# Weight sums made by accumulating transfers in DRAM, kept first-layer sums, other signs, and a new order of work

## The chip, the cores and the metric

The kernel runs on one core of one Trainium2 chip. A core has TensorE (PE in the profile, with PEld for the loading of its weights), VectorE (DVE), ScalarE (ACT), GpSimd (POOL) and SyncE (SP), which issues most of the transfers; sixteen DMA engines carry them. The metric is the time on the device in microseconds, the median of several runs. Before the change it is 613.53 us (three runs, 613.44 to 614.0).

## The reference

Input x has 2048 rows of 640 numbers in float32. Two branches are computed from it and mixed by a gate for each row:

```
qkv  = x @ wqkv                      # 32 heads of 20
o    = attention over 8 earlier rows at distances 0, 2, .. 14
a    = o @ wo
h    = x @ w1 + b1                   # 640 -> 1728
b    = (h * tanh(softplus(h))) @ w2  # mish, 1728 -> 640
g    = sigmoid((x * gate_w).sum(-1))
out  = g * a + (1 - g) * b
```

## The kernel before

**Arithmetic.** Each float32 operand is split into a high part that TensorE multiplies at full rate and a low part; a product is then three matmuls, high by high, high by low, low by high (`mm3`, lines 534 to 536). The split is one ACT instruction (line 466) and one subtraction on DVE or POOL (line 469). A buffer with the two halves is called a pair.

**Fewer products.** Most products are done in 2 by 2 blocks with seven products in place of eight (the Winograd form of Strassen's scheme). It needs sums and differences of blocks of the left and of the right operand. They are written t1 to t4 for activations and s1 to s4 for weights. Of a weight in blocks 11, 12, 21 and 22 there are four combinations.

- First layer (x times w1): the 2048 rows are worked in two halves, P = 0 and 1, and w1 in six groups q of columns. `pieces` loads the weights of one group and sums them on DVE or POOL (lines 1096 to 1100 and 1125 to 1128, by the helper at line 1044). In the first half the class Quad pairs two blocks of rows of the weight at once, in the second half Single pairs one. `KIND = 'SSSSSS'` makes all six groups Single in the second half. Each has the steps first, second, m1 to m4, l1 and l2, one PSUM bank or more each.
- qkv: eight units u of columns and rows, with eight slots each; unit 2 and 3 together are done by the class Two in the seven-product form (`PAIRS = {2: (0, 1)}`, `load_first` and `load_second`, steps a1 to c3).
- Second layer (mish times w2), `mlp2`: seven products a, b, c, e, g, d, f (`PRODUCTS`), each over seven blocks kc of 128 rows. Its weights are w2's blocks and their sums. `load_step` loads those of a step at least three steps ahead.
- Output product (o times wo), `wo_part`, for both halves with the same seven products and a fifth block of rows ("+" and "-", weights taken positive or negated).

**The weight sums of the last two products.** `sums_of` is called nine times, once for each of seven blocks of w2 and two of wo, where the order of work has the token `sum`. It loads three buffers of weights, makes three sums (lines 1266 and 1279) and a small fourth one on DVE or POOL and a negated part on ACT (line 1285), and stores five pieces to DRAM (`s_d`, `so_d`), from which `load_step` and `load_weights` read them later. The signs of these sums are such that "b" of the output product, the last step of "b" of the second layer and the fifth block of wo also need negated weights (`load_minus`, `load_stack` with minus, `load_minus_two`).

**Accumulating transfers.** A DMA issued on POOL can add to what lies at its target. The kernel before does so for sums of activations: `plus` (line 955) and `adding` (line 1554, in `wo_part`).

**Who sets the order.** The kernel is written as tasks, each for one engine, with what they wait for and which buffers they take. `Plan.run` plays them through with estimated durations and fixes each engine's order; on the chip each engine then goes through its own list in order and waits where something is not there yet. Tasks for "ANY" go to DVE or POOL. Buffers come from rings and are handed out in the order in which the tasks were made. That order is the text ORDER (lines 260 to 274), a list of tokens such as `q.1.0.l2` or `u.4.7`. BANKS (line 259) says which of two rings of PSUM banks a step uses. Attention runs on DVE beside all of this (lines 591, 594, 637, 641) until the middle of the second layer.

Of the kernel before, what the change touches and what calls it, by code (L numbers as in the profile page):

```python
# [259 lines left out]
ORDER = """  # L260
u.0.5 u.0.4 u.0.7 u.0.6 q.0.0.first wq.1 q.0.0.m1 q.0.0.second sum q.0.0.m3 last.0 q.0.0.m4 u.1.0 u.1.2 pieces.0.1 pieces.0.2 q.0.0.l1 q.0.1.first
u.1.1 q.0.1.second q.0.1.m1 sum q.0.0.m2 q.0.0.l2 wa.2 q.0.2.first q.0.1.m4 q.0.1.m3 u.1.3 u.1.7 u.1.5 q.0.1.m2 pieces.0.3 last.1 q.0.1.l1 q.0.1.l2
p.2.0.a1 u.1.6 u.1.4 pieces.0.4 q.0.2.second x.2.4 q.0.2.m1 x.3.1 q.0.2.m3 p.2.3.a1 p.2.0.a2 q.0.2.m2 p.2.1.a1 p.2.0.a3 pieces.0.5 q.0.2.m4 q.0.2.l2
q.0.2.l1 p.2.2.a1 p.2.1.a2 p.2.3.a2 p.2.2.a2 p.2.1.a3 p.2.3.a3 q.0.3.first x.3.4 p.2.0.b2 p.2.1.b2 p.2.1.b1 q.0.3.m1 p.2.2.a3 p.2.3.b2 p.2.0.b1
q.0.3.m4 p.2.3.b1 q.0.3.second p.2.2.b1 q.0.3.m3 q.0.4.first q.0.3.m2 q.0.4.m1 q.0.3.l2 q.0.3.l1 q.0.4.second p.2.0.c0 q.0.4.m2 q.0.4.m3 p.2.2.c0
x.3.2 x.2.0 p.2.2.b2 wc.2 q.0.5.first q.0.4.m4 q.0.4.l2 q.0.5.m1 p.2.1.c0 q.0.4.l1 x.2.1 p.2.0.c1 p.2.2.c1 p.2.3.c0 x.3.0 q.0.5.m2 p.2.2.c3 q.0.5.m4
q.0.5.l2 q.0.5.second p.2.3.c1 p.2.3.c3 p.2.0.c3 x.2.3 x.2.2 p.2.0.c2 p.2.1.c1 p.2.1.c3 q.0.5.m3 third wq.4 x.3.3 p.2.3.c2 q.0.5.l1 p.2.1.c2 p.2.2.c2
u.4.7 u.4.5 u.4.0 pieces.1.0 rest.0 u.4.6 forms.1.0 sum wq.5 u.4.2 sum u.4.3 q.1.0.first q.1.0.second q.1.0.m1 u.4.1 u.4.4 pieces.1.1 q.1.0.m4
q.1.0.m3 q.1.0.l1 u.5.6 u.5.2 u.5.5 u.5.7 u.5.1 q.1.1.first rest.1 u.5.0 sum pieces.1.2 q.1.1.m1 q.1.0.l2 q.1.0.m2 q.1.1.second wq.6 sum wq.7 u.5.4
q.1.1.m4 q.1.1.m3 u.5.3 q.1.2.first q.1.2.m2 u.6.0 pieces.1.3 u.6.2 q.1.1.l1 q.1.2.m1 q.1.2.second u.6.1 q.1.2.m3 u.6.4 q.1.1.l2 q.1.2.m4 u.6.3 u.6.6  # L270
q.1.3.first q.1.1.m2 u.6.7 u.6.5 pieces.1.4 q.1.2.l2 u.7.4 u.7.1 q.1.3.second q.1.4.first q.1.3.m1 q.1.3.m4 u.7.3 u.7.2 q.1.3.m2 sum u.7.5 sum u.7.7
q.1.3.m3 q.1.2.l1 q.1.4.m1 u.7.6 q.1.3.l1 sum q.1.3.l2 q.1.4.second q.1.4.m4 pieces.1.5 q.1.4.m2 lastw.1 u.7.0 q.1.4.m3 q.1.5.first q.1.4.l2 q.1.5.m1
q.1.5.second q.1.4.l1 q.1.5.m4 q.1.5.m3 rest.2 q.1.5.m2 q.1.5.l2 q.1.5.l1 last.2 last.3 rest.3
# [4 lines left out]
def kernel(ctx: ExitStack, tc: tile.TileContext, x, wq, wo, w1, b1, w2, out):  # L278
# [125 lines left out]
    s_d = [dram.tile([128, 1280], F32, name=f"s{kc}") for kc in range(KH)]  # L404
# [726 lines left out]
    def last_pieces(P):  # L1131
# [7 lines left out]
        if P:  # L1139
            W1["second"] = ws  # L1140
# [864 lines left out]
```

## Time and profile before

| | us |
|---|---|
| median of three runs | 613.53 |
| the profiled execution | 614.11 |
| its span, first to last instruction | 612.3 |
| PE busy | 608.3 |
| DVE busy | 578.6 |
| ACT busy | 387.4 |
| POOL busy | 354.9 |

The span is what the trace covers; the execution is 1.8 us longer. Busy times of engines overlap, so they are compared with the span, not added. Two further lines of the page show how the time is spread over the span, each digit the busy tenths of one of forty slices of 15.3 us:

```profile
DVE  8799998999999999999999999999999999989956
POOL 1666799978788915464579566686359864001000
```

POOL is used until the attention on DVE has ended and hardly after that, since the planner gives tasks for "ANY" to DVE from there on. The transfers use the sixteen DMA engines for 0.78 of the span on the mean, at 240 GB/s. In the views of single lines, an entry such as `x8: 779/815/1143` gives the number of instructions and their shortest, median and longest time in ns.

### The profile page before, as it was taken

How to read it: one execution, taken by the hardware profiler on the slowest of the kernel's cores; microseconds unless marked ns; L12 is line 12 of the kernel's file. 1: busy time of each engine (PE TensorE's matmuls, PEld its weight loads, DVE VectorE, ACT ScalarE, POOL GpSimd, SP SyncE). 2: the span in 40 equal slices, each digit the busy share in tenths (PEclk: the TensorE clock that was granted, in tenths of full speed). 3: DMA queues.
4: the chain of work that ended last, by engine and by line, in shares of the span. 5: the costliest groups of instructions: out<-in, count | busy, mean ns of one | idle time of the engine just before them, and what ended most of it. 6: DMA issues, size and time to landing. Idle time of an engine off the chain costs nothing.

```text
span 612.3 us, 9208 instructions
## 1 busy us (share of the span) xinstructions
PE 608.3 (99%) x2710; PEld 505.7 (83%) x2710; DVE 578.6 (94%) x517; ACT 387.4 (63%) x887; POOL 354.9 (58%) x334
## 2 busy tenths in 40 slices
PE   9999999999999999999999999999999999999997
PEld 7888888888888888888888888888888888888886
DVE  8799998999999999999999999999999999989956
ACT  7678567766897575666656775784966653736520
POOL 1666799978788915464579566686359864001000
PEclk9999999999999999999999999999999999999999
DMA  9764796749788688876888799989798874979913
GB/s 323 227 206 139 239 280 194 269 150 313 278 288 262 188 235 221 257 235 185 225 243 277 226 318 284 346 236 267 232 329 239 231 226 140 279 251 303 279 65 120
DMA packets 101346, 147.01 MB, mean 240 GB/s; under 512 B 11616, under 2 KB 54624, under 8 KB 101072
## 3 DMA queue, kind: packets, MB, share of 16 engines
q1 hardware_dynamic: 97936, 140.66, 71.1%
q0 software_dynamic: 3072, 5.51, 6.4%
q8 instruction: 21, 0.34, 0.3%
q14 instruction: 29, 0.24, 0.1%
q10 hardware_dynamic: 288, 0.26, 0.1%
HBM read 92.38 MB, written 53.03 MB: 237 GB/s over the span
## 4 chain that ended last, share of the span: by engine, by line
PE 97%; ACT 1%; DVE 1%; issue 0%; POOL 0%
PE qb L534 16%; PE qb L535 16%; PE qb L536 16%; PE sb L535 16%; PE sb L536 16%; PE sb L534 16%; PE qb L698 1%; DVE raw L1044 1%; ACT pair L466 1%; PE sb L442 1%; PE sb L540 0%; PE qb L541 0%; PE sb L541 0%; PE qb L540 0%; POOL raw L1044 0%
## 5 line engine op out<-in xcount | busy, mean ns | idle before, releaser
L469 POOL TENSOR_TENSOR pair<-raw,pair 128x512 fp32r<-128x512 f32 (+3 forms) x136 | 169.5, 1269 | 69.0 <-ACT pair L466 46.9
L466 ACT ACTIVATE pair<-raw 128x512 fp32r<-128x512 f32 (+3 forms) x235 | 137.1, 611 | 53.9 <-DMA raw<-actt 12.6
L536 PE MATMUL sb<-pair,pair 128*128 128x512 f32 (+1 forms) x396 | 153.0, 386 | 0.0
L534 PE MATMUL sb<-pair,pair 128*128 128x512 f32 (+1 forms) x396 | 153.0, 386 | 0.0
L535 PE MATMUL sb<-pair,pair 128*128 128x512 f32 (+1 forms) x396 | 153.0, 386 | 0.0
L534 PE MATMUL qb<-pair,pair 128*128 128x512 f32 (+1 forms) x377 | 145.6, 386 | 0.0
L535 PE MATMUL qb<-pair,pair 128*128 128x512 f32 (+1 forms) x377 | 145.5, 386 | 0.0
L536 PE MATMUL qb<-pair,pair 128*128 128x512 f32 (+1 forms) x377 | 145.4, 386 | 0.0
L591 DVE TENSOR_TENSOR pr<-kvq,qg 128x2560 f32<-128x2560 f32 x32 | 89.8, 2807 | 3.3 <-ACT qg L597 2.3
L637 DVE TENSOR_TENSOR pr<-kvq,pg 128x2560 f32<-128x2560 f32 x32 | 90.2, 2820 | 1.0
L594 DVE TENSOR_REDUCE lg<-pr 128x128 f32<-128x2560 f32 x32 | 90.2, 2818 | 0.7
L641 DVE TENSOR_REDUCE kvq<-pr 128x320 f32<-128x2560 f32 x32 | 90.0, 2814 | 0.4
L534 PEld LDWEIGHTS sb<-pair,pair 128*128 128x128 f32 x396 | 74.3, 188 | 14.9
L535 PEld LDWEIGHTS sb<-pair,pair 128*128 128x128 f32 x396 | 74.3, 188 | 14.8
L536 PEld LDWEIGHTS sb<-pair,pair 128*128 128x128 f32 x396 | 74.3, 188 | 14.7
L534 PEld LDWEIGHTS qb<-pair,pair 128*128 128x128 f32 x377 | 70.8, 188 | 14.4 <-ACT qb L1171 0.5
L536 PEld LDWEIGHTS qb<-pair,pair 128*128 128x128 f32 x377 | 70.8, 188 | 13.8
L535 PEld LDWEIGHTS qb<-pair,pair 128*128 128x128 f32 x377 | 70.8, 188 | 13.7
L469 DVE TENSOR_TENSOR pair<-raw,pair 128x512 fp32r<-128x512 f32 (+3 forms) x99 | 68.6, 714 | 3.7 <-ACT pair L466 3.5
L1044 POOL TENSOR_TENSOR hb<-hb,hb 128x512 f32<-128x512 f32 x42 | 55.0, 1327 | 11.7 <-ACT hb L1177 4.8
L1044 POOL TENSOR_TENSOR raw<-raw,raw 128x128 f32<-128x128 f32 (+3 forms) x49 | 40.5, 840 | 12.9 <-DMA raw<-in_wq 2.9
L469 POOL TENSOR_TENSOR pair<-hb,pair 128x512 fp32r<-128x512 f32 (+2 forms) x29 | 34.9, 1210 | 15.7 <-DMA act<-hb 5.8
(173 smaller groups left out, 755.1 us busy)
## 6 DMA issues: line engine op xcount, KB each, us to landing
actt<-hb SPq DMA_DIRECT2D x52, 256.0 KB, 4.0
raw<-in_w SPq DMA_DIRECT2D x40, 256.0 KB, 4.0
act<-hb SPq DMA_DIRECT2D x38, 256.0 KB, 4.2
raw<-actt SPq DMA_DIRECT2D x37, 256.0 KB, 2.6
raw<-in_wq SPq DMA_DIRECT2D x36, 248.0 KB, 4.0
raw<-act SPq DMA_DIRECT2D x29, 256.0 KB, 4.4
raw<-in_x SPq DMA_DIRECT2D x27, 256.0 KB, 4.0
o<-ot SPq DMA_DIRECT2D x64, 80.0 KB, 3.2
```

The source lines that it names most:

```text
L442: nc.tensor.matmul(warm_banks[i % 3].t[:, :n], ones[:, :128], ones[:, :n], start=i < WARM, stop=True, skip_group_check=True)
L466: a = add("ACT", act_ns(n), lambda: A.activation(hi(), raw(), AF.Copy), after, rank=rank, take=take, hold=hold)
L469: return (V if e == "DVE" else G).tensor_tensor(lo(), raw(), hi().bitcast(F32), op=OP.subtract)
L534: nc.tensor.matmul(ps, ah, bh, start=first, stop=False, skip_group_check=more)
L535: nc.tensor.matmul(ps, ah, bl, start=False, stop=False, skip_group_check=more)
L536: nc.tensor.matmul(ps, al, bh, start=False, stop=last, skip_group_check=more)
L591: return V.tensor_tensor(pr, window(kv, s0, 0), qg[:, :, None, :].to_broadcast([128, 2, W, QF]), op=OP.mult)
L594: V.tensor_reduce(lg_w[:, s0:s0 + 2], pr.rearrange("p s w (h d) -> p s w h d", d=DH), op=OP.add, axis=AX.X)
L637: V.tensor_tensor(pairs.rearrange("p s k i (h d) -> p s k i h d", d=DH), vw, pg[:, s0:s0 + 2].rearrange("p s (k i) h -> p s k i h", i=2)[: ...
L641: V.tensor_reduce(q[:, s0:s0 + 2], pairs.rearrange("p s k i f -> p s f k i"), op=OP.add, axis=AX.XY)
L698: nc.tensor.matmul(ps.t[:, :n], X[0, kc].t[:, a, i * 128:(i + 1) * 128], WQ[0, kc].t[:, b, :n], start=a == b and kc == 0, stop=False)
L1044: return (V if e == "DVE" else G).tensor_tensor(t.t[:, i:i + n], a.t[:, j:j + n], b.t[:, k:k + n], op=op)
```

## The change

1. `sums_of` is a new function. For each of w2 and wo it makes four tensors that cover all blocks at once, each with one copy from DRAM to DRAM on SP's queue and one accumulating DMA on POOL's queue. The nth is started when a PE task has ended: for w2 the step l2 of the second half's group n - 1, for wo the nth product of the second layer. The tokens `sum` that are left in ORDER do nothing.
2. w2 and wo are laid out anew by the host (two halves; 256 columns of all blocks, then 128, then 256), wo's fifth block is an input of its own, wo4. A weight block of 384 columns is then two DMAs of 256 and 128 columns (`load_parts`, `block`).
3. The signs of the sums are others. t3 and t4 of the second layer's activations are turned round, several additions of the second layer and of `wo_part` become subtractions and the reverse, and the negated fifth block of wo is dropped; "d" and "f" of the output product and one step of "d" and "f" of the second layer take negated weights in its place. After the second layer's "d", DVE reads the PSUM bank itself, where ACT copied it to a buffer before.
4. The first half's `pieces` stores its sums to DRAM, and the second half's loads them in place of making them (four sums of 128 columns for each group). The same is written for the class Two (`keep`, `kept_raw`), for a unit 6 in PAIRS, which PAIRS does not have.
5. ORDER and BANKS are new.

```diff
 ORDER = """
-u.0.5 u.0.4 u.0.7 u.0.6 q.0.0.first wq.1 q.0.0.m1 q.0.0.second sum q.0.0.m3 last.0 q.0.0.m4 u.1.0 u.1.2 pieces.0.1 pieces.0.2 q.0.0.l1 q.0.1.first
+u.0.5 pieces.0.1 u.0.7 q.0.0.first u.0.6 u.0.4 wq.1 q.0.0.second q.0.1.first last.0 u.1.1 q.0.1.m1 pieces.0.2 wa.2 q.0.0.m1 pieces.0.3 q.0.0.m2
...
-    s_d = [dram.tile([128, 1280], F32, name=f"s{kc}") for kc in range(KH)]
+    s_d = {n: dram.tile([128, KH * (256 if n == 1 else 384)], F32, name=f"s{n}") for n in (1, 2, 3, 4)}
...
-        if P:
+        if P and KIND[q] == "S":
             ra, rb, rc = [raw_buf() for _ in range(3)]
...
-            dc = dma(lambda: rc.t[:, 256:384], lambda: w1[b][:, 0], take=[rc], size=65536)
-            s1 = combined(128, (rc, 384), (rc, 256), (rb, 128), OP.add, [db, dc], rank=SOON)
-            s3 = combined(128, (rc, 256), (ra, 0), (rc, 256), OP.subtract, [da, s1], rank=SOON)
-            s2 = combined(128, (rc, 0), (rc, 384), (ra, 0), OP.subtract, [da, s1], rank=SOON)
-            s4 = combined(128, (rc, 128), (ra, 256), (rc, 0), OP.subtract, [s2], rank=SOON)
-            PIECES[P, q] = [split_pair(ra, 512, [da]), split_pair(rb, 512, [db]), split_pair(rc, 512, [s4, s3])]
+            dc = dma(lambda: rc.t, lambda: w1s_d[q, 0], kept_sums[q], take=[rc])
+            PIECES[P, q] = [split_pair(ra, 512, [da]), split_pair(rb, 512, [db]), split_pair(rc, 512, [dc])]
...
+                kept_sums[q] = [dma(lambda i=i: w1s_d[q, 0][:, i * 256:(i + 1) * 256].rearrange("p (k f) -> p k f", f=128),
+                                    lambda r=r: r.t.rearrange("p (k f) -> p k f", f=256)[:, :, :128], w, rank=1.0, hold=[r], size=131072)
+                                for i, r, w in ((0, o1, [s4]), (1, rb, [s3]))]
...
+    def let_go(P, q, t):
+        if P and q < 4:
+            sums_of(w2, KH, s_d, "s", 1 + q, t)
...
+    def sums_of(w, k, to, key, n, at):
+
+        a1, a1r, a2 = k * 256, k * 384, k * 640
+        first = {1: lambda: w[0][:, a1r:a2], 2: lambda: w[0][:, :a1r], 3: lambda: w[0][:, :a1r], 4: lambda: w[1][:, :a1r]}[n]
+        more, wide = {1: (lambda: w[1][:, a1r:a2], a1), 2: (lambda: to[1], a1), 3: (lambda: w[0][:, a1r:a2], a1), 4: (lambda: to[2], a1r)}[n]
+        c = dma(lambda: to[n], first, [at], rank=0.5, size=512 * (a1 if n == 1 else a1r))
+        before = done[key, n // 2] if n % 2 == 0 else []
+        done[key, n] = [add("POOL", 900, lambda: G.dma_start(out=to[n][:, :wide], in_=more(), accum_op=OP.add, max_dma_last_dim=2048), [c] + before,
+                            rank=-0.5, size=1024 * wide, late=1500)]
+
+    def load_parts(srcs, after=(), minus=False, wide=True):
...
+    def block(of, k, i):
+
+        return [(256, lambda: of()[:, i * 256:(i + 1) * 256]), (128, lambda: of()[:, k * 256 + i * 128:k * 256 + (i + 1) * 128])]
...
                     elif name == "d":
-                        z = stage(True)
-                        read["v", P, j] = c = copy(z, bank["v", P, j], [ends["d", "v", P, j]], [z])
                         b = zw[key]
-                        v = two("ANY", b, b, z, OP.add, [c, b.done])
-                        y[key].used = v = two("ANY", b, y[key], b, OP.subtract, [v, y[key].done])
+                        read["v", P, j] = v = two("DVE", b, bank["v", P, j], b, OP.subtract, [ends["d", "v", P, j], b.done])
+                        y[key].used = v = two("ANY", b, y[key], b, OP.add, [v, y[key].done])
                         result(b, 2 * P + 1, 2 + j, [v])
...
+                if k < 4:
+                    sums_of(wo, 2, so_d, "so", 1 + k, last)
...
     def load_last_weights():
-        weights["-"] = load_minus_two([lambda: wo[4][:, :256], lambda: wo[4][:, 384:]])
-        weights["+"] = load_two([lambda: wo[4][:, :256], lambda: wo[4][:, 384:]], [])
-        weights["4"] = load_pair(lambda: wo[4][:, 256:384], "ANY", n=128, wide=True)
+        weights["+"] = load_parts([(256, lambda: wo4[:, :256]), (256, lambda: wo4[:, 384:])])
+        weights["4"] = load_pair(lambda: wo4[:, 256:384], "ANY", n=128, wide=True)
...
         def l2(self):
             t = self.mms(self.de, self.one(1, 1, self.form("t4")) + self.plain(1, 0), [self.sd])
+            let_go(self.P, self.q, t)
             self.acted(1, 0, self.de, [t])
...
-        elif kind == "sum":
-            sums_of(*sums_left.pop(0))
```

More of the change, by code (lines that the diff above doesn't have):

```diff
@@ L265 @@
[L265 to L268, printed above, removed]
@@ L274, with kernel @@
+q.1.4.m1 q.1.3.l1 q.1.4.m4 q.1.4.m3 q.1.3.l2 sum q.1.4.l2 q.1.5.first q.1.5.second sum wq.7 q.1.5.m2 u.7.2 q.1.5.m1 u.7.7 u.7.3 q.1.4.l1 q.1.4.m2 sum
+q.1.5.m4 q.1.5.l2 lastw.1 last.2 q.1.5.m3 q.1.5.l1 u.7.5 u.7.1 last.3 rest.1 u.7.6 u.7.4 u.7.0 rest.2 rest.3
 """
 @with_exitstack
-def kernel(ctx: ExitStack, tc: tile.TileContext, x, wq, wo, w1, b1, w2, out):
+def kernel(ctx: ExitStack, tc: tile.TileContext, x, wq, wo, wo4, w1, b1, w2, out):
     nc = tc.nc
@@ L803, in plain_weights, with keep, kept_raw @@
                 self.w["r", half, kc] = split_pair(r, n, [d])
+        def keep(self, name, i, r, after):
+            if self.P or i not in PAIRS.get(6, ()):
+                return []
+            kept_sums[name, i] = [dma(lambda: wqs_d[name, i][:, :NCOL], lambda: r.t[:, :NCOL], after, rank=1.0, hold=[r], size=NCOL * 512)]
+            return kept_sums[name, i]
+        def kept_raw(self, name, i):
+            r = raw_buf()
+            self.w[name, i] = split_pair(r, self.n, [dma(lambda: r.t[:, :NCOL], lambda: wqs_d[name, i][:, :NCOL], kept_sums[name, i], take=[r], size=NCOL * 512)])
         def load_first(self):
@@ new lines, in load_parts, with parts @@
+    def load_parts(srcs, after=(), minus=False, wide=True):
+        raw, p, n = stage(wide), pair_buf(), sum(m for m, _ in srcs)
+        def parts():
+            at = 0
+            for m, src in srcs:
+                nc.sync.dma_start(raw.t[:, at:at + m], src())
+                at += m
+        d = add("SP", 450 * len(srcs), parts, after, take=[raw], size=n * 512)
+        if minus:
+            a = add("ACT", act_ns(n), lambda: A.activation(p.t[:, 0, :n], raw.t[:, :n], AF.Copy, scale=-1.0), [d], rank=SOON, take=[p], hold=[raw])
+            b = add("DVE", dve_ns(n), lambda: V.scalar_tensor_tensor(p.t[:, 1, :n], raw.t[:, :n], -1.0, p.t[:, 0, :n].bitcast(F32),
+                    op0=OP.mult, op1=OP.subtract), [a], rank=SOON, hold=[raw, p])
+            p.ready = [a, b]
+        else:
+            p.ready = split(lambda: raw.t[:, :n], lambda: p.t[:, 0, :n], lambda: p.t[:, 1, :n], n, [d], "ANY", [raw], [p], SOON)
+        return p
@@ L1459, in after_product @@
                         z = y[key] = zp[key]
-                        z.done = two("DVE", z, z, bank["u", P, j], OP.add, [ends["c", "u", P, j], z.done])
+                        z.done = two("DVE", z, bank["u", P, j], z, OP.subtract, [ends["c", "u", P, j], z.done])
                     elif name == "e":
@@ L1475, in after_product @@
                         b = y[key]
-                        result(b, 2 * P, 2 + j, [two("DVE", b, b, bank["v", P, j], OP.subtract, [ends["f", "v", P, j], b.used])])
+                        result(b, 2 * P, 2 + j, [two("DVE", b, b, bank["v", P, j], OP.add, [ends["f", "v", P, j], b.used])])
                 if name in "bd":
@@ L1732, in wo_part @@
         for j in range(2):
-            y[j].done = two("DVE", y[j], y[j], bank[f"u{j}"], OP.add, [ends[f"u{j}"], y[j].done])
+            y[j].done = two("DVE", y[j], bank[f"u{j}"], y[j], OP.subtract, [ends[f"u{j}"], y[j].done])
         for j in range(2):
```

206 lines of the change are left out of this document (87 added, 119 removed).

## The prediction

> **What bounds the kernel now.** The page comes first, its head and its first part (busy time, share of the span, number of instructions). Then the busy time of each engine by stage: a row has the stretch, its length, then busy us and number of instructions of PE, PEld, DVE, ACT and POOL, the granted clock, the share of the DMA engines and GB/s.
>
> ```profile
> span 612.3 us, 9208 instructions
> PE 608.3 (99%) x2710; PEld 505.7 (83%) x2710; DVE 578.6 (94%) x517; ACT 387.4 (63%) x887; POOL 354.9 (58%) x334
> ```
>
> ```profile
> 60.00:220.00 160.00, 160.00 (x714) 133.44 (x713) 153.73 (x106) 111.89 (x283) 129.13 (x114) 1.00 0.77 245
> 220.00:378.00 158.00, 158.00 (x709) 132.86 (x708) 154.57 (x112) 102.54 (x244) 97.45 (x101) 1.00 0.83 245
> 378.00:434.00 56.00, 56.00 (x249) 46.37 (x248) 54.85 (x40) 38.44 (x79) 35.96 (x32) 1.00 0.90 275
> 434.00:546.00 112.00, 112.00 (x495) 92.74 (x495) 108.96 (x121) 65.56 (x134) 57.67 (x50) 1.00 0.79 239
> 546.00:580.00 34.00, 34.00 (x151) 28.15 (x150) 33.39 (x57) 19.59 (x35) 2.49 (x3) 1.00 0.96 289
> ```
>
> TensorE is busy for the whole of every stage at a granted clock of 1.00. DVE stands close behind, but it is not what ends last. A busy PE need not be a PE at its pace, so the next view is PE's timeline (start, length, line, tiles, shape) at the only places where two matmuls start more than 0.26 us apart once the start-up is over.
>
> ```profile
> 35.11 0.39 PE L536 MATMUL sb<-pair,pair 128*128 128x512 f32 x1
> 35.55 0.50 PE L534 MATMUL qb<-pair,pair 128*128 128x512 f32 x1
> 35.89 0.40 PE L535 MATMUL qb<-pair,pair 128*128 128x512 f32 x1
> 36.12 0.39 PE L536 MATMUL qb<-pair,pair 128*128 128x512 f32 x1
> ```
>
> ```profile
> 75.66 0.38 PE L535 MATMUL qb<-pair,pair 128*128 128x496 f32 x1
> 75.88 0.38 PE L536 MATMUL qb<-pair,pair 128*128 128x496 f32 x1
> 76.24 0.50 PE L534 MATMUL qb<-kvq,pair 128*128 128x512 f32 x1
> 76.58 0.39 PE L535 MATMUL qb<-kvq,pair 128*128 128x512 f32 x1
> ```
>
> ```profile
> 146.97 0.39 PE L536 MATMUL qb<-pair,pair 128*128 128x512 f32 x1
> 147.33 0.50 PE L534 MATMUL qb<-kvq,pair 128*128 128x512 f32 x1
> 147.67 0.40 PE L535 MATMUL qb<-kvq,pair 128*128 128x512 f32 x1
> ```
>
> The pace is the distance of two starts: 36.12 - 35.89 = 0.23 us for 512 columns, 75.88 - 75.66 = 0.22 us for 496. From 35.11 to 35.89 two steps took 0.78 us instead of 0.45, so 0.33 us were lost. From 75.88 to 76.58 it was 0.70 instead of 0.45, and from 146.97 to 147.67 the same: 0.25 us each. **All the waiting of PE after its start is 0.33 + 0.25 + 0.25 = 0.83 us.** The view of waits names what ended the three:
>
> ```profile
> PEld qb L534 <- ACT qb L1171: 0.5, 1, 0.5
> PEld qb L534 <- ACT hb L1177: 0.4, 1, 0.4
> PEld qb L534 <- ACT hx L708: 0.4, 1, 0.4
> ```
>
> Each time a weight load waited for an ACT instruction that had to read a PSUM bank first. No wait for a DMA, for POOL or for DVE reaches PE. What is left of the span lies behind the last matmul:
>
> ```profile
> 608.91 0.28 PE L536 MATMUL qb<-pair,pair 128*128 128x256 f32 x1
> 609.23 0.42 DVE L1707 TENSOR_TENSOR kvq<-kvq,qb 128x256 f32<-128x256 f32 x1 [0.54 <-PE qb L536]
> ```
>
> From 609.2 to 612.3 the last half block is added and sent: 3.1 us, in the order that the change also has.
>
> So the time is PE's stream plus its ends. The profiled execution took 614.11 us, 1.8 more than its span; the median of the three runs is 613.53, that is 0.58 below the profiled one. I take the same 0.58 off any sum.
>
> **The change, part by part.**
>
> *PE.* The edits touch neither mm3 (lines 534 to 536) nor mm2 (540, 541), nor PRODUCTS, KIND and PAIRS, which set how many products there are. A ("-", ...) becomes ("+", ...) with the same matmul. 2710 matmuls remain, of the same widths: 0 us. A gain can only come out of the 0.83 us, so the best case is 613.53 - 0.83 = 612.7 us. That is 0.14% and less than the 0.2% (1.23 us) which a measurement of this kernel can tell from no change.
>
> *Weight sums off POOL.* These are two answers of the busy time over the whole span for single lines: 1266, then 1279, the sums of w2 and wo. Behind them stand the 128x128 sums of the second half's pieces (from the groups: number, busy us, mean ns, idle time before them).
>
> ```profile
> 0.00:613.00 613.00, 18.00 (x27) 1.00 0.78 240
> 0.00:613.00 613.00, 11.97 (x9) 1.00 0.78 240
> ```
>
> ```profile
> L1044 POOL TENSOR_TENSOR raw<-raw,raw 128x128 f32<-128x128 f32 x19 | 8.8, 476 | 6.3 <-DMA actt<-hb 2.3 <-DVE hb L1044 1.6 <-DVE ot L547 1.3
> L1044 DVE TENSOR_TENSOR raw<-raw,raw 128x128 f32<-128x128 f32 x5 | 2.0, 406 | 0.0
> ```
>
> POOL loses 18.0 + 12.0 + 8.8 = 38.8 us of its 354.9, DVE 2.0 us, and ACT nine small negations. POOL is 58% busy and releases no matmul late, so this is worth 0 on the path: the 99% of PE hides it. Were PE not there, DVE with 94% would be next, and it loses only the 2.0 us.
>
> *Accumulating transfers.* In their place come four copies on SP's queue and four accumulating DMAs on POOL's for w2, and as many small ones for wo. The issue of such a DMA on POOL, and its time from issue to landing:
>
> ```profile
> L1554 POOL DMA_DIRECT2D ot<-ot x8: 779/815/1143, 239.3 to 571.4; - x8
> DMA to landing us min/median/max: 4.0/5.7/7.7
> ```
>
> These move 128x512 (0.262 MB). The new ones move 1792, 1792, 1792 and 2688 columns for w2 (4.13 MB) and 512, 512, 512 and 768 for wo (1.18 MB). No row shows an issue of that size. Low end: a fixed 0.81 us each, 6.5 us for eight. High end: in step with the bytes, 5.31 / 0.262 x 0.81 = 16.4 us. Nothing excludes either; I take 8 us, near the row, as the rows differ in partitions but not in time. POOL still ends with 22 to 32 us less work.
>
> *DMA engines.* The queues' rows give prices:
>
> ```profile
> q1 hardware_dynamic: 97936, 140.66, 71.1%
> q0 software_dynamic: 3072, 5.51, 6.4%
> ```
>
> Two rows of the sums' tensor, their stores and the first loads of a sum (number, ns min/median/max, first and last start in us), place them in time:
>
> ```profile
> L499 SPq DMA_DIRECT2D s<-raw x35: 319/382/1905, 42.7 to 319.1; - x35
> L1320 SPq DMA_DIRECT2D hb<-s x5: 377/430/1179, 408.0 to 447.8; - x5
> ```
>
> On q1 1 MB costs 0.711 x 612.3 / 140.66 = 3.1 us of all sixteen engines, on q0, which only accumulates, 0.064 x 612.3 / 5.51 = 7.1 us. Removed: nine times 0.655 MB in and out, 11.8 MB, 36.5 us. Added: accumulates 5.31 MB x 7.1 = 37.7 us; copies 6.49 MB x 3.1 = 20.1 us; twelve stores of 0.131 MB for the kept pieces and six loads longer by 0.197 MB, 2.75 MB, 8.5 us. Net +30 us in 612, so the mean share goes from 0.78 to about 0.83. The sums of w2 now all fall into the second half of the first layer (row 220:378, share 0.83) instead of being spread from 42.7 us on. The largest accumulate is 1.38 MB, 9.8 us of all engines. A load of SP's queue that shares them for all of that time can land up to 10 us late.
>
> What hides this: in the second layer loads run three steps ahead, and a step is 18 matmuls of 0.227 us, 4.1 us, so 12 us. The sums themselves are not urgent: they start when a PE task of the second half ends, and the first load of one was issued at 408.0 us.
>
> The Trainium skill says on this point, in "DMA: Bandwidth & Descriptors", section "Issuing engines are not separate DMA queues", that DMAs of all issuing engines end on the same 16 engines and interleave. By that rule the accumulates take turns with the loads, which is the contention above; no row of this trace isolates it.
>
> *SP's queue.* 72 issues go (nine sums with three loads and five stores). 8 copies, 12 stores and 24 further issues for weights that are now read in two blocks come. 28 fewer, so the queue gains slack: 0.
>
> *Signs.* The second layer's "d" loses four ACT copies to DVE reading the bank itself; wo loses one negated weight. This follows the product's end and no matmul waits for it in the trace: 0. The bank is read by DVE instead of ACT, and DVE is fuller. The end of this is that a bank could come free late, by one DVE instruction of 2.8 us at most (attention's), but attention is over by then:
>
> ```profile
> 511.93 2.82 DVE L641 TENSOR_REDUCE kvq<-pr 128x320 f32<-128x2560 f32 x1
> ```
>
> *keep and kept_raw* act only if PAIRS has a unit 6. It has not: 0.
>
> *The new list* sets another order of all PE work in the first layer and other PSUM rings. Its cost is the waits at its own hand-overs. The low end is none (-0.83 us). The high end is what several waits of the seen size or one long one make: ten of 0.3 us are +3 us. The nearest rows are the three waits, so I take about as many, 0.7 us.
>
> **Sum:** 613.53 - 0.83 + 0.7 = 613.4 us.
>
> **The rivals.**
>
> 1. *POOL stands still for a copy (slower).* The accumulate sits in POOL's queue and waits there for its copy, and everything behind it on POOL, above all the low halves of line 469 that PE multiplies by, waits too. The trace has such waits:
>
> ```profile
> POOL o L1554 <- DMA o<-ot: 45.3, 1, 45.3
> POOL actt L955 <- DMA act<-hb: 6.3, 1, 6.3
> ```
>
> The long one falls after 512 us, when nothing else was put on POOL, so it cost nothing. A copy of 1.38 MB takes 4.3 us alone and 8 to 9 beside equal traffic. This decides once the wait is longer than the lead of the low halves queued behind it, some 4 us for one step. Then three copies of this size with 1 us too much each give +3 us, 616.4. Against it: POOL has 42% idle, and the mean of its work per us falls. Chance 0.14.
>
> There is a rule that would make this worse: the Trainium skill, "SBUF — State Buffer", section "SBUF: two separate sides", says that while DVE runs an instruction which takes the port shared with GpSimd, GpSimd can't write descriptors. By it each of eight issues would wait for one DVE instruction of 2.82 us, 22 us of POOL. The trace does not agree: issues took 0.779 to 1.143 us beside a DVE that is 94% busy. So it does not raise the chance.
>
> 2. *The list waits at other places (slower).* ACT releases PE at all three waits; in another order a bank is read late more often. It decides from five further waits of 0.25 us (1.25 us). Six to eight give 615. Against it: three in 2710 matmuls is what the order before shows. Chance 0.11.
>
> 3. *Faster by over 0.2%.* It would need 1.23 us, where 0.83 are to be had. Only a shorter tail or start could add to it, and neither is edited. Chance 0.03, about 612.2.
>
> 4. *The change does not do what it says* (the sums land as before in effect, only elsewhere): then nothing moves on PE, 613.5. It falls together with the forecast.
>
> **How the numbers follow.** The forecast, PE's stream unchanged and waits under 2 us in all, has 0.72: 613.4 us, by itself 612.7 to 614.7. Slower is 0.14 + 0.11 = 0.25, faster 0.03. The range goes from the floor, 612.7, up to 616.0, which takes in the list's rival and the nearer half of POOL's; outside stay some 0.03 below and 0.12 above.
>
> **What would show it.** Right: PE still has 2710 matmuls and about 608 us busy; no gaps of over 0.26 us beyond a handful; POOL falls to about 325 us; q0 grows to about 10.8 MB and 12 to 13% of the engines. Wrong: waits of PE for POOL's low halves (line 469) right behind an accumulate; or waits for DMA between 220 and 378 us. The forecast would be wrong at its root if the span fell below 611.5 us, as PE's stream itself would then have become shorter.

## The result, and the profile after

| | before | after |
|---|---|---|
| median, us | 613.76 (613.44 to 614.3, 4 runs) | 618.15 (617.88 to 618.51, 4 runs) |
| ratio | | 1.0071, 95% interval 1.0054 to 1.0088 |
| profiled execution, us | 614.11, span 612.3 | 618.51, span 616.7 |

The changed kernel is 4.4 us slower. That is outside the predicted range (612.7 to 616.0) and on the other side of its 613.4. The page of the changed kernel, its head and its two queues:

```profile
span 616.7 us, 9053 instructions
...
PE 609.4 (99%) x2710; PEld 504.7 (82%) x2710; DVE 579.1 (94%) x516; ACT 392.3 (64%) x879; POOL 322.9 (52%) x282
...
q1 hardware_dynamic: 91728, 137.84, 68.1%
q0 software_dynamic: 5984, 10.82, 11.4%
```

PE has the same 2710 matmuls and is busy for about as long, and POOL lost 32 us: the work is what was foreseen. The busy time by stage (start and end, length, busy us of PE, PEld, DVE, ACT, POOL, granted clock, DMA share, GB/s) shows where PE is not filled any more:

```profile
20.00:60.00 40.00, 38.62 (x169) 31.09 (x168) 32.05 (x30) 25.75 (x60) 24.00 (x21) 1.00 0.65 198
60.00:220.00 160.00, 158.26 (x701) 130.91 (x700) 157.50 (x110) 116.00 (x281) 109.95 (x92) 1.00 0.74 232
220.00:378.00 158.00, 158.00 (x708) 132.72 (x708) 154.33 (x106) 104.27 (x243) 81.14 (x69) 1.00 0.88 249
434.00:546.00 112.00, 112.00 (x496) 92.78 (x495) 110.90 (x127) 69.09 (x139) 54.64 (x49) 1.00 0.92 284
```

The stages in which the accumulating transfers run, from 220 us on, are full, although their DMA share rose (0.83 to 0.88, and 0.79 to 0.92 in the last row). The two stages ahead of them are not. The view of waits of PE's weight loads names who released it (us in total, times, longest); the start-up and two rows of 0.2 us are left out:

```profile
PEld sb L537 <- ACT sb L936: 1.5, 2, 1.1
PEld sb L539 <- DVE pair L472: 1.2, 1, 1.2
PEld qb L537 <- DVE hb L1234: 0.9, 1, 0.9
PEld sb L537 <- DVE sb L883: 0.9, 1, 0.9
PEld sb L537 <- ACT hb L997: 0.7, 1, 0.7
PEld qb L537 <- ACT qb L1216: 0.7, 1, 0.7
PEld sb L538 <- POOL pair L472: 0.4, 1, 0.4
```

Before there were three such rows, of 0.4 and 0.5 us, all for ACT. (Lines 534 to 536 are now 537 to 539, low half 469 is 472, high half 466 is 469, sum 1044 is 1074.)

To add them up I counted, in PE's timeline from 6 us on, each place where two matmuls start more than 0.26 us apart, as the distance less a pace of 0.225 us. This table holds that count, in us, for every trace that is spoken of below (in brackets the number of the experiment):

| kernel | 6 to 60 us | 60 to 90 | 90 to 160 | 160 to 200 | from 200 | all |
|---|---|---|---|---|---|---|
| before | 0.32 | 0.25 | 0.24 | 0 | 0 | 0.8 |
| after | 2.21 | 0.80 | 0.11 | 2.22 | 0 | 5.3 |
| after, no stores (1) | 1.69 | 0.80 | 0.10 | 2.21 | 0 | 4.8 |
| after, no accumulating sums (2) | 2.44 | 0 | 0.08 | 2.21 | 0 | 4.7 |
| after with the old list (3) | 0 | 0 | 3.05 | 5.95 | 29.20 | 38.2 |
| before with the new list (4) | 1.12 | 0.75 | 0.77 | 17.53 | 16.48 | 36.7 |
| after, early sums on DVE (5) | 0.18 | 0.98 | 0.10 | 2.22 | 0 | 3.5 |
| before, a multiplication twice (6) | 4.85 | 0 | 0.25 | 0 | 0 | 5.1 |
| after, a multiplication twice (7) | 4.92 | 0.81 | 0.10 | 2.22 | 1.24 | 9.3 |
| after, no stores, early sums on DVE (8) | 0.16 | 0.83 | 0.10 | 2.21 | 0.52 | 3.8 |
| after, no multiplication at 163 us (9) | 3.81 | 0 | 0 | 1.48 | 0 | 5.3 |
| after, no stores (10) | 1.80 | 0 | 0.10 | 2.21 | 1.06 | 5.2 |
| after, as 5 and 9, copy of line 936 on DVE (11) | 0.45 | 0.72 | 0.10 | 2.71 | 0 | 4.0 |

From before to after 4.5 us came up, against 4.4 us between the two profiled executions. The match is closer than the count deserves: the first 6 us lie outside it, and the start differs from trace to trace. The 85th matmul starts at 20.61 us before and at 19.93 us after, and among the variants of the changed kernel between 19.85 and 20.98 us. **There are two places: up to 90 us, +2.4 us, and 167 to 185 us, +2.2 us.** Behind 185 us the changed kernel's PE never waits. The second place came out at 2.21 or 2.22 us in all seven traces that leave list, code and work there as they are (after, 1, 2, 5, 7, 8 and 10). The first is not as steady: experiments 2 and 9 issue the same instructions as the changed kernel up to 160 us, and lost 2.4 and 3.8 us up to 90 us where it lost 3.0.

**The first place.** PE's timeline (start, length, line, tiles, shape, in brackets the idle time before it and who ended it):

```profile
38.08 0.50 PE L539 MATMUL sb<-kvq,pair 128*128 128x512 f32 x1 [0.76 <-DVE pair L472]
...
43.01 0.50 PE L537 MATMUL qb<-pair,pair 128*128 128x512 f32 x1 [0.31 <-ACT qb L1216]
...
48.38 0.50 PE L537 MATMUL sb<-pair,pair 128*128 128x512 f32 x1 [0.31 <-ACT hb L997]
```

DVE's timeline at that place, then POOL's and ACT's:

```profile
34.44 4.73 DVE L472 TENSOR_TENSOR pair<-raw,pair 128x512 fp32r<-128x512 f32 x5
41.04 1.31 DVE L472 TENSOR_TENSOR pair<-raw,pair 128x512 fp32r<-128x512 f32 x1 [1.87 <-issue]
42.27 2.81 DVE L594 TENSOR_TENSOR pr<-kvq,qg 128x2560 f32<-128x2560 f32 x1
```

```profile
36.41 3.35 POOL L1074 TENSOR_TENSOR raw<-raw,raw 128x256 f32<-128x256 f32 x3
...
47.36 0.74 POOL L1074 TENSOR_TENSOR raw<-raw,raw 128x256 f32<-128x256 f32 x1
```

```profile
39.80 1.15 ACT L469 ACTIVATE pair<-raw 128x512 fp32r<-128x512 f32 x2 [2.66 <-POOL raw L1074]
...
41.36 0.44 ACT L600 ACTIVATE qg<-kvq 128x320 f32<-128x320 f32 x1
...
42.34 0.61 ACT L1216 ACTIVATE qb<-sb 128x512 f32<-128x512 f32 x1
```

Five low halves take DVE 0.95 us each, and three sums take POOL 1.12 us each, while both run; another such sum took POOL 0.74 us. PE, at 37 us, waits for one of the five. ACT stands for 2.66 us until POOL's sums are done, then the copy of line 600 and the seed of line 1216 (the copy into the PSUM bank from which PE goes on) come behind, and PE waits for that seed at 43 us. The third wait, at 48 us, is for ACT's instruction of line 997. A fourth, at 79 us (0.69 us, the row of line 1234), is for a sum of DVE; it is missing in experiments 2, 9 and 10. The first multiplication of attention starts at 42.27 us. Before it was here:

```profile
35.13 2.81 DVE L591 TENSOR_TENSOR pr<-kvq,qg 128x2560 f32<-128x2560 f32 x1
```

**The second place**, ACT's timeline and the matmul that waited:

```profile
165.59 0.68 ACT L1222 ACTIVATE hb<-sb,bias 128x512 f32<-128x512 f32 x1
166.16 1.63 ACT L469 ACTIVATE pair<-raw 128x496 fp32r<-128x496 f32 x3
167.68 0.58 ACT L936 ACTIVATE sb<-pair 128x496 f32<-128x496 f32 x1
```

```profile
168.32 0.49 PE L537 MATMUL sb<-pair,pair 128*128 128x496 f32 x1 [0.64 <-ACT sb L936]
...
172.01 0.49 PE L537 MATMUL sb<-pair,pair 128*128 128x496 f32 x1 [0.53 <-DVE sb L883]
```

The copy that seeds PE's bank (line 936) has no idle time of ACT ahead of it: three high halves stand in the queue before it. 3.7 us later PE waits again, for a subtraction of DVE, and at 185 us for 0.20 us, again for a copy of line 936.

### The profile page after: what moved, and what is told of

Read it like the earlier page. It is cut to its first block, busy times and chain, and to the rows that moved or that the text cites. A ratio compares the mean times of both kernels' runs of the same rounds, so it can differ in the third digit from the quotient of the medians.

```text
span 616.7 us, 9053 instructions
## 1 busy us (share of the span) xinstructions
PE 609.4 (99%) x2710; PEld 504.7 (82%) x2710; DVE 579.1 (94%) x516; ACT 392.3 (64%) x879; POOL 322.9 (52%) x282
## 4 chain that ended last, share of the span: by engine, by line
PE 88%; DVE 6%; DMA 2%; ACT 1%; issue 1%; POOL 1%; SPq 0%; POOLq 0%; DVEq 0%
PE sb L537 15%; PE sb L538 15%; PE sb L539 15%; PE qb L537 13%; PE qb L538 13%; PE qb L539 13%; DVE lg L597 2%; DVE pr L594 2%; DVE pair L472 1%; DMA raw<-in_wq 1%; DMA raw<-in_w 1%; POOL raw L1074 1%; PE qb L701 1%; DVE pr L640 0%; DVE hb L1234 0%
## 5 line engine op out<-in xcount | busy, mean ns | idle before, releaser
L472 POOL TENSOR_TENSOR pair<-raw,pair 128x512 fp32r<-128x512 f32 (+3 forms) x133 | 167.8, 1287 | 101.7 <-ACT pair L469 59.8
L469 ACT ACTIVATE pair<-raw 128x512 fp32r<-128x512 f32 (+3 forms) x230 | 135.5, 613 | 71.4 <-DMA raw<-actt 11.9
L537 PE MATMUL sb<-pair,pair 128*128 128x512 f32 (+1 forms) x406 | 157.3, 387 | 1.5 <-ACT sb L936 0.6
L538 PE MATMUL sb<-pair,pair 128*128 128x512 f32 (+1 forms) x406 | 156.9, 386 | 0.0
L539 PE MATMUL sb<-pair,pair 128*128 128x512 f32 (+1 forms) x406 | 156.8, 386 | 0.0
L537 PE MATMUL qb<-pair,pair 128*128 128x512 f32 (+2 forms) x367 | 141.9, 387 | 0.3 <-ACT qb L1216 0.3
L538 PE MATMUL qb<-pair,pair 128*128 128x512 f32 (+2 forms) x367 | 141.7, 386 | 0.0
L539 PE MATMUL qb<-pair,pair 128*128 128x512 f32 (+2 forms) x367 | 141.7, 386 | 0.0
L537 PEld LDWEIGHTS sb<-pair,pair 128*128 128x128 f32 x406 | 76.2, 188 | 18.2 <-ACT sb L936 1.5
L538 PEld LDWEIGHTS sb<-pair,pair 128*128 128x128 f32 x406 | 76.2, 188 | 15.2 <-POOL pair L472 0.4
L539 PEld LDWEIGHTS sb<-pair,pair 128*128 128x128 f32 x406 | 76.2, 188 | 15.0
L537 PEld LDWEIGHTS qb<-pair,pair 128*128 128x128 f32 x367 | 68.9, 188 | 14.5 <-ACT qb L1216 0.7
L539 PEld LDWEIGHTS qb<-pair,pair 128*128 128x128 f32 x367 | 68.9, 188 | 13.5
L538 PEld LDWEIGHTS qb<-pair,pair 128*128 128x128 f32 x367 | 68.9, 188 | 13.4
L472 DVE TENSOR_TENSOR pair<-raw,pair 128x512 fp32r<-128x512 f32 (+2 forms) x97 | 70.5, 755 | 6.2 <-ACT pair L469 4.1
L1074 POOL TENSOR_TENSOR hb<-hb,hb 128x512 f32<-128x512 f32 x44 | 57.1, 1314 | 27.9 <-DVE pg L630 8.9
L469 ACT ACTIVATE pair<-hb 128x512 fp32r<-128x512 f32 (+3 forms) x63 | 37.6, 598 | 12.0 <-DMA hb<-in_w 4.8
```

The lines of the kernel that those rows point to most:

```text
L469: a = add("ACT", act_ns(n), lambda: A.activation(hi(), raw(), AF.Copy), after, rank=rank, take=take, hold=hold)
L472: return (V if e == "DVE" else G).tensor_tensor(lo(), raw(), hi().bitcast(F32), op=OP.subtract)
L537: nc.tensor.matmul(ps, ah, bh, start=first, stop=False, skip_group_check=more)
L538: nc.tensor.matmul(ps, ah, bl, start=False, stop=False, skip_group_check=more)
L539: nc.tensor.matmul(ps, al, bh, start=False, stop=last, skip_group_check=more)
L1074: return (V if e == "DVE" else G).tensor_tensor(t.t[:, i:i + n], a.t[:, j:j + n], b.t[:, k:k + n], op=op)
```

## The experiments

Theories: **the list** (A), the new order of PE's work makes hand-overs that DVE and ACT serve too late; **the transfers** (B), the new stores or accumulates hold back a load, POOL or SP; and within A, **lateness** (A1: DVE is behind, and PE pays for it) against **the hand-over itself** (A2: it is too tight whether DVE is behind or not).

**1. Without the stores of the first-layer sums.**

```diff
-            dc = dma(lambda: rc.t, lambda: w1s_d[q, 0], kept_sums[q], take=[rc])
+            dc = dma(lambda: many(rc), lambda: w1[b][:, :4], kept_sums[q], take=[rc])
...
+                kept_sums[q] = [add("SP", 450, lambda: None, w, rank=1.0, hold=[r], size=131072) for r, w in ((o1, [s4]), (rb, [s3]))]
```

> The changed kernel, with every engine's order of work as it is, but the twelve stores of kept first-layer sums are planned and not issued; the second half's loads read w1 itself in their place (so its first layer is computed from other weights). After the change PE loses about 2.2 us between 36.9 and 48.4 us, right behind the first two stores. If those stores cause it, by holding raw buffers which the loads of x for the forms need next, these gaps shrink to under 0.7 us and the time is about 616.3 us. If the list causes it, the gaps stay and the time is 618.1 us, as after the change. The waits around 167 to 172 us stay by both theories.

617.27 us (616.95 to 618.29), ratio 1.0051 [1.0034, 1.0068]. It lies between, and its interval overlaps that of the change. In its trace two of the three waits up to 60 us are gone, and the first, for the low half, grew from 0.93 to 1.39 us.

**2. Without the accumulating sums.**

```diff
-        c = dma(lambda: to[n], first, [at], rank=0.5, size=512 * (a1 if n == 1 else a1r))
+        c = add("SP", 450, lambda: None, [at], rank=0.5, size=512 * (a1 if n == 1 else a1r))
...
-        done[key, n] = [add("POOL", 900, lambda: G.dma_start(out=to[n][:, :wide], in_=more(), accum_op=OP.add, max_dma_last_dim=2048), [c] + before,
+        done[key, n] = [add("POOL", 900, lambda: None, [c] + before,
```

> The changed kernel with every engine's order as it is, but the eight copies and eight accumulating transfers of the weight sums are planned and not issued; the second layer and the output product read plain blocks of w2 and wo in the place of the sums. If the accumulating transfers cost time (POOL standing still behind a copy, or loads sharing the DMA engines), the time falls towards 614 to 616 us and waits of PE after 185 us go away. If the list costs it, 618.1 us as after the change, since all of PE's waits lie before 185 us and the first transfer of the sums starts later.

618.38 us (617.62 to 618.86), ratio 1.007 [1.0055, 1.0085]: as with them. **5.3 MB of accumulates and their copies cost nothing that these runs can tell**, and in the changed kernel PE has no wait behind 185 us that they could have caused; the first copy is issued at 228 us.

**3 and 4. Each list with the other code.** The edit exchanges ORDER and BANKS.

> The changed kernel with ORDER and BANKS of before. If the code is free and the new list alone costs the 4.4 us, this gives 613 to 614 us. If the code costs them, 618 us. If a list fits only the code that it was made for, both theories on single parts fail and it is far above 618 us, 625 us or more, with waits of PE all over the first layer.

> The kernel before with ORDER and BANKS of the change. If the new list alone costs the 4.4 us, this gives about 618 us. If the code does, 613.5 us. If a list fits only the code that it was made for, it is far above 618 us, 625 us or more.

652.11 us and 650.3 us, one run each. The first is 34 us over the changed kernel, the second 36.5 us over the one before, so the totals don't divide the 4.4 us between code and list. They show that a list fits the code that it was made for.

Up to 90 us the traces do divide it. With the old list PE loses 0.57 us there under the old code and nothing under the new one; with the new list it loses 1.87 us under the old code and 3.01 us under the new one. Attention begins on DVE at 35.13 and 33.68 us with the old list, at 40.76 and 42.27 us with the new one. These are its first multiplications in experiment 3, then in 4:

```profile
33.68 2.81 DVE L594 TENSOR_TENSOR pr<-kvq,qg 128x2560 f32<-128x2560 f32 x1
```

```profile
40.76 2.82 DVE L591 TENSOR_TENSOR pr<-kvq,qg 128x2560 f32<-128x2560 f32 x1 [0.35 <-ACT qg L597]
```

**So the first place comes with the new list, whichever code runs under it** (one trace each). Six of the twelve stores of first-layer sums are issued before 60 us under the old list too, and PE waits for nothing. Behind 90 us the two runs wait at places of their own, so whether list or code makes the second place stays open.

**5. The early combinations on DVE alone.**

```diff
-                    ins = t.fn(e) if t.both else t.fn()
+                    ins = t.fn("DVE" if e == "POOL" and now < 41000 else e) if t.both else t.fn()
```

> The changed kernel with the same order of work, but what POOL does of additions and low halves before about 41 us is issued on DVE at the same place of the order. After the change DVE instructions with two operands take 1.2 to 1.8 us where a POOL instruction runs beside them and 0.69 alone, and the attention on DVE begins at 42.3 us, 35.1 before. Theory A: this mutual hold-up in the first 42 us sets how late DVE is from then on, and PE's waits up to 185 us follow from it. Then DVE's early instructions fall to 0.69 us, the attention begins 2 to 3 us earlier, PE's waits shrink by 1 to 2 us and the time is 616 to 617 us. Theory B: the list's waits have nothing to do with DVE being late: 618.1 us. Theory C: DVE, with more to do, becomes later still: over 619 us.

616.95 us (616.64 to 618.46), ratio 1.0055 [1.004, 1.007]. The groups of 8 to 42 us by form (number, busy us, mean ns, idle time before), first in the changed kernel, then here:

```profile
L472 DVE TENSOR_TENSOR pair<-raw,pair 128x512 fp32r<-128x512 f32 x19 | 17.4, 956 | 5.6 <-ACT pair L469 3.7 <-issue 1.9
```

```profile
L472 DVE TENSOR_TENSOR pair<-raw,pair 128x512 fp32r<-128x512 f32 x22 | 14.5, 688 | 5.4 <-ACT pair L469 5.4
L1074 DVE TENSOR_TENSOR raw<-raw,raw 128x512 f32<-128x512 f32 x8 | 5.5, 688 | 0.2
```

With POOL out of the way a low half takes 688 ns instead of 956, and DVE does more of them in less time. Attention begins earlier, and PE's waits up to 60 us fall from 2.21 to 0.18 us:

```profile
38.85 2.82 DVE L594 TENSOR_TENSOR pr<-kvq,qg 128x2560 f32<-128x2560 f32 x1
```

So lateness is what PE pays for up to 60 us; 0.18, 0.16 and 0.45 us in the three traces with this edit (5, 8 and 11) stand against 1.69 to 3.81 us in the five without it (after, 1, 2, 9 and 10). The edit takes away two latenesses at once, DVE's slow low halves and POOL's sums that ACT stood still for, and does not divide them. The Trainium skill, "SBUF — State Buffer", section "SBUF: two separate sides", says that a DVE instruction with two SBUF inputs and a GpSimd instruction that reads SBUF exclude each other. The 688 and 956 ns agree that they hold each other up, not that they exclude each other wholly: in the 2.76 us from 36.41 to 39.17 us, when both ran, about 2.9 low halves and 2.5 sums were done, 3.8 us of work by 0.688 and 0.74 us each (my estimate from the rows above), and there the measurement decides. But the hold-up isn't what the change added. Before had the same hold-up, in the same view of 8 to 42 us:

```profile
L469 DVE TENSOR_TENSOR pair<-raw,pair 128x512 fp32r<-128x512 f32 x15 | 12.9, 869 | 1.9 <-ACT pair L466 1.6
L1044 DVE TENSOR_TENSOR raw<-raw,raw 128x512 f32<-128x512 f32 x5 | 6.7, 1348 | 0.0
```

That is 15 x 0.18 + 5 x 0.66 = 6.0 us of DVE lost, against 19 x 0.27 = 5.1 us after. The old list had the room for it. Of the 7.14 us by which attention begins later (42.27 against 35.13), 3.42 went with POOL's work; 3.72 us stay, and experiments 3 and 4 give them to the new order.

**6 and 7. A multiplication of attention twice**, the first one, in the kernel before and in the changed one.

```diff
-                return V.tensor_tensor(pr, window(kv, s0, 0), qg[:, :, None, :].to_broadcast([128, 2, W, QF]), op=OP.mult)
+                for _ in range(2 if (u, s0) == (0, 6) else 1):
+                    ins = V.tensor_tensor(pr, window(kv, s0, 0), qg[:, :, None, :].to_broadcast([128, 2, W, QF]), op=OP.mult)
+                return ins
```

> The kernel before with the first attention multiplication on DVE issued twice, 2.82 us more on DVE at 35 us and nothing else. Theory A: the order of before has less room than that, PE then waits as after the change, mostly between 70 and 190 us: 615.5 to 617.5 us. Theory B, waits come from the list's places and not from a late DVE: 613.5 to 614 us.

> The changed kernel with the first attention multiplication issued twice, 2.82 us more on DVE at 42 us. Theory A: there is no room left, so nearly all of it reaches PE: 620 to 621.5 us. Theory B: 618 to 618.5 us.

617.45 us (617.02 to 618.15), ratio 1.0056 [1.0039, 1.0073], and 623.48 us in one run: 2.8 us more on DVE cost 3.7 and 5.3 us, the second more than either theory had. Part of the 3.7 is a TensorE clock that dropped right after the wait (last section), 1.6 us in the profiled run; the run at a full mean clock took 617.02 us, 3.3 more. Of the second, 1.24 us came up at 346 us. The kernel before with its old list now shows how it reaches PE; ACT's timeline, then PE's (599 and 1173 are lines 597 and 1171):

```profile
40.70 0.44 ACT L599 ACTIVATE qg<-kvq 128x320 f32<-128x320 f32 x1 [3.37 <-DVE pr L592]
41.08 0.55 ACT L1173 ACTIVATE qb<-qb 128x512 f32<-128x512 f32 x1
```

```profile
41.68 0.50 PE L534 MATMUL qb<-pair,pair 128*128 128x512 f32 x1 [2.63 <-ACT qb L1173]
```

ACT's next query copy must wait until DVE has read the last one, and the seed that PE needs stands behind it in ACT's queue. **DVE's lateness at the start of attention goes to PE through ACT.** In the second place nothing moved: 2.22 us with DVE earlier (5) and later (7). That is against lateness carried over from the start.

**8 and 10. No stores, with the early sums on DVE, and no stores once more for its trace.** The edits are those of 1 and 5.

> The changed kernel with the two earlier edits together: the first-layer weight sums are not stored and not read back (the second half multiplies by columns of the weights themselves, so these products are left out of the computation), and before 41 us DVE does the combinations that the plan had given to POOL. Alone the first took the time from 618.15 to 617.27 us, the second to 616.95. If both act through the same lateness of DVE in the first 60 us, they do not add: 616.3 to 617.0, and PE's waits up to 60 us stay near 0.2 us as with the second alone. If the stores cost by something of their own (the transfers' share of the DMA engines, SP's queue), the gains add: 0.9 + 1.2 us, about 616.0, with the difference beyond 60 us. The 2.2 us of waits between 160 and 200 us should stay in both cases.

> The first-layer sums not stored and not read back, as in the run of 617.27 us, once more for its trace. Where do the 0.9 us come from? If SP's stores and the DMA engines delay what the first products wait for, PE's waits up to 90 us fall from 3.0 to about 2 us while DVE's shared-port durations stay (1.2 to 1.8 us before 42 us). If the difference lies elsewhere (start-up before 6 us, or after the last matmul), the waits stay at 3.0 us and the first or last matmul is about 0.9 us earlier.

617.25 us (616.45 to 618.02), ratio 1.0061 [1.0044, 1.0078], not below the 616.95 of the early sums alone, and 618.01 us in one run. The gains don't add. In experiment 10's trace PE's waits up to 90 us were 1.80 us instead of 3.0, as B expects, yet 1.06 us came up at 431 us, for a low half of POOL. Nor is the difference up to 90 us clear: without the stores it is 2.5 and 1.8 us (1 and 10), with them 3.0, 2.4 and 3.8 us (after, 2 and 9). What the stores cost by themselves stays open, between nothing and 0.9 us.

**9. Without the attention multiplication at 163 us.**

```diff
+                if (u, s0) == (1, 0):
+                    return
                 V.tensor_tensor(pairs.rearrange("p s k i (h d) -> p s k i h d", d=DH), vw,
```

> The changed kernel without one attention multiplication on DVE (2.8 us, the one that starts at 163 us; its product is left out of the computation). It asks what holds PE for 2.22 us between 167 and 185 us. If it is DVE being behind at that place, DVE's part of these waits goes (the 0.7 us at 171 us and the 0.2 us at 185 us, each for a DVE subtraction of line 883), while the first wait, for ACT's copy of line 936 behind three high halves, stays at about 0.8 us: PE loses 1.0 to 1.3 us there instead of 2.22, and the time is about 617.1. If the hand-over itself is too tight in the new list (PE's products, a PSUM bank, ACT and DVE in turn), with DVE not the late one, the waits stay at 2.2 us and the time at 618.1.

617.87 us (617.24 to 618.63), ratio 1.007 [1.0055, 1.0085]. All waits of PE that this trace has, but for the start-up (938 and 885 are lines 936 and 883):

```profile
PEld sb L539 <- DVE pair L472: 2.3, 1, 2.3
PEld sb L537 <- ACT sb L938: 1.5, 2, 1.1
PEld sb L537 <- DVE sb L885: 0.4, 1, 0.4
```

Between 160 and 200 us 2.22 us became 1.48: the wait for DVE's subtraction shrank from 0.69 to 0.16 us, ACT's copy kept its 0.80 us and the wait at 185 us its 0.20. That one had been counted as DVE's; it is ACT's, one of the two in the second row, and so less went than the 1.0 to 1.3 us that were to be left. So a third of the second place is DVE being behind there, and the rest is not. The time hardly shows it, since two of the four runs took 618.5 us and the profiled one of them lost 3.81 us up to 60 us (last section); the other two took 617.24 and 617.28 us.

**11. The copy of line 936 by DVE**, on top of 5 and 9.

```diff
-            s = add("ACT", act_ns(n) + 60, lambda: A.activation(ga.t[:, :n], ut()[:, :n], AF.Copy), [du], rank=-0.5, take=[ga], hold=[ga, u])
+            s = add("ACT", act_ns(n) + 60, lambda: V.tensor_copy(ga.t[:, :n], ut()[:, :n]) if 165000 < plan.now < 165600
+                    else A.activation(ga.t[:, :n], ut()[:, :n], AF.Copy), [du], rank=-0.5, take=[ga], hold=[ga, u])
```

> The changed kernel with the early combinations on DVE, without the attention multiplication at 163 us (its product is left out), and with one more edit: the copy of line 936 that PE waited for at 167 us is done by DVE instead of ACT. In the run without the multiplication alone PE lost 1.48 us between 160 and 200 us, 0.80 of it at this copy. If the copy was late because it stood in ACT's queue behind three high halves, DVE starts it up to 1 us earlier, the 0.80 us falls to 0.3 or less and the sum there to 0.6 to 1.0 us: about 615.7 us. If the bank or the load of u comes free only then, the copy starts no earlier whoever does it, and the sum stays at 1.4 to 1.6 us: about 616.3 us. In both cases the waits up to 60 us stay near 0.2 us and those from 60 to 90 us near 0.9 us.

619.21 us (618.16 to 619.93), ratio 1.009 [1.0072, 1.0108]: neither. The trace is of the run of 618.16 us; the three others ran at a mean clock of 0.996 or 0.997, and no trace of them was kept. DVE's timeline (647 and 939 are lines 644 and 936) says what went wrong at the copy:

```profile
165.51 2.81 DVE L647 TENSOR_REDUCE kvq<-pr 128x320 f32<-128x2560 f32 x1
168.25 0.67 DVE L939 COPY sb<-pair 128x496 f32<-128x496 f32 x1
```

The copy now stood behind a reduction of 2.81 us, and PE's wait at it grew from 0.80 to 2.29 us. So the question that it was to answer, queue or bank, is not answered; that ACT's queue is the cause rests on the unbroken row of ACT at 166.16 us and is argued only. What it does show is that one instruction's place in an engine's order is worth 1.5 us of PE here.

No kernel among these beats the one before; the fastest with the new list took 616.95 us.

## Why the prediction was wrong

- *PE's stream unchanged*: right. 2710 matmuls, at the old pace wherever PE doesn't wait (0.2240 us a step on the mean, before 0.2239).
- *Weight sums off POOL, worth 0*: right. POOL was to fall to about 325 us and has 322.9. That it bought nothing is what 99% of PE had said.
- *Accumulating transfers, 8 us of POOL and 0 on the path*: right. Their eight issues, from the view of line 1302 (number, ns min/median/max, first and last start):

```profile
L1302 POOL DMA_DIRECT2D s<-in_w x2: 1273/1275/1277, 236.3 to 297.9; - x2
L1302 POOL DMA_DIRECT2D s<-s x2: 1115/1204/1292, 282.6 to 334.9; - x2
L1302 POOL DMA_DIRECT2D so<-in_wo x2: 803/812/822, 420.8 to 466.7; - x2
L1302 POOL DMA_DIRECT2D so<-so x2: 844/850/855, 445.6 to 486.1; - x2
```

Twice the medians make 8.3 us, and experiment 2 prices them at nothing. Rival 1, POOL standing still for a copy, had its mechanism but no victim. In the waits of POOL (the first ended with DVE, but its copy had landed only 0.7 us earlier, at 297.25 us):

```profile
POOL s L1302 <- DVE pr L640: 7.0, 1, 7.0
...
POOL so L1302 <- DMA so<-in_wo: 2.9, 1, 2.9
```

No matmul was late behind either. Nor did the issues wait out an instruction of DVE, which rival 1 weighs at 22 us: the one at 420.81 us took 0.82 us inside a reduction from 419.31 to 422.12 us, the one at 334.93 us took 1.12 us inside a multiplication from 333.71 to 336.53 us.

- *DMA +30 us of all engines, hidden*: hidden, but half the size. q1 went from 0.711 x 612.3 = 435 us to 0.681 x 616.7 = 420, q0 from 39 to 70: +16 us. The bytes came as foreseen (q1 -2.8 MB, q0 +5.3 MB); the price of 1 MB, which the prediction took from before, fell from 7.1 to 6.5 us on q0 and from 3.10 to 3.05 on q1.
- *Signs, SP's queue, keep, each 0*: nothing in the trace speaks against it, as PE doesn't wait where the signs changed, and SP has 28 issues fewer (665, before 693), as foreseen; they were not tried one by one. The twelve stores of first-layer sums, which the prediction had under the DMA engines and SP's queue, may cost up to 0.9 us.
- *The new list*: "The nearest rows are the three waits, so I take about as many, 0.7 us". **This step failed.** It measured 5.3 us. What came was rival 2 in kind, waits at other places, and there the size failed as well: I had a unit of 0.25 us and 615 us for six to eight of them. There were seven of 0.20 to 0.93 us, 4.3 us together, and 1.1 us of smaller ones behind them; three of the seven were for DVE, which had released PE at none of the three before. Three waits in the old order were taken as a rate, as if an order had a rate of waits. They were what was left by a list that fits its code, as the 34 and 36.5 us of experiments 3 and 4 show; and up to 90 us those two give the new waits to the list (1.87 and 3.01 us, against 0.57 and 0 with the old one). What makes the second place, 2.2 us, is shown for a third only. And the step "ACT releases PE at all three waits" stopped at the last releaser. Further back stands DVE, as experiment 6 shows for the start of attention, and it is nearly full there. The busy time of the kernel before in the stretch of 20 to 60 us, of which the prediction has no row:

```profile
20.00:60.00 40.00, 39.95 (x178) 32.86 (x177) 38.48 (x32) 28.66 (x74) 27.03 (x25) 1.00 0.61 187
```

DVE is busy for 38.48 of 40 us while PE loses 0.3 us. Experiment 6 is the price of that: 2.8 us more there cost 3.7 us of 613.75. After the change DVE is busy for only 32.05 us of this stretch (the first row of the stages after): it is late there without being full, and stood 3.7 us between 8 and 42 us until ACT had high halves ready (1.6 us before). A new order at a place where the old one had no slack had an upper end of several us, not of 3.

## What to carry to other kernels

A change that brings a new order of work is priced by its order first, even where every instruction that it adds or removes is hidden: look for the stretches where the second engine is over 95% busy, and ask by how much each hand-over to the bound engine is ahead there. A few small waits in a tuned order are no rate for another order. Follow a wait at least two steps back: the releaser (ACT) may itself stand behind a copy that waits for the engine that is really late (DVE).

## What the hardware showed that was not expected

After some waits PE ran at half its rate. In experiment 9 and in experiment 6, by stretch:

```profile
36.00:43.50 7.50, 5.58 (x18) 4.11 (x18) 7.50 (x7) 6.15 (x16) 5.38 (x6) 0.77 0.68 212
```

```profile
42.00:46.50 4.50, 4.50 (x14) 3.55 (x13) 4.40 (x3) 1.22 (x3) 3.99 (x5) 0.62 0.27 83
```

The granted clock falls to 0.77 and 0.62 over these few us: eight matmuls start 0.43 us apart instead of 0.23, 1.6 us lost beyond the wait itself. Idle times of 1.93 us (at 37.4 us, experiment 9) and 2.63 us (at 38.7 us, experiment 6) led to it; one of 2.85 us (at 48.5 us, experiment 7) didn't, nor did one of 1.93 us before the same matmul in experiment 2, which issues the same instructions up to there. From 36.0 to 43.5 us that trace has 25 matmuls at a clock of 1.00, experiment 9's has 18. The Trainium skill, "TensorE: Matmul & The Clock Gate", Part 1, gives an idle window of about 3.4 us, free-running, after which the array runs at half its clock. That it depends on more than the wait's length agrees; that 1.93 us can be enough does not, and there the measurement decides. It makes the time of one kernel jump: of experiment 9's four runs, the two at a mean clock of 0.997 are about 1.3 us longer than the two at 1.00.
